# The first layer's last five pairs of blocks of batches 1 to 7 in 128x128 products, behind K0 to K2

## The chip, the cores and the metric

The kernel runs on one core of one Trainium2 chip. What counts is the device time of one execution in microseconds, taken as the median of several runs. A core has TensorE (PE; its weight loads are shown apart as PEld), VectorE (DVE), ScalarE (ACT), GpSimd (POOL) and SyncE (SP, which here only issues DMAs). Each engine takes its own instructions in a fixed order, and they wait for each other by semaphores.

## The reference

Attention with normalised queries and keys, and behind it two layers of a perceptron with a tanh GELU between them:

```python
q_n, k_n = rmsnorm(q, g_q), rmsnorm(k, g_k)          # (8, 12, 448, 64)
scores = scale * (q_n @ k_n.transpose(0, 1, 3, 2))
attn = softmax(scores)                               # over the keys
x = (attn @ v).transpose(0, 2, 1, 3).reshape(3584, 768)
h = x @ w_in                                         # 768 -> 2048
g = gelu_tanh(h)
out = g @ w_out                                      # 2048 -> 768, float32
```

## The kernel before

The work goes batch by batch, eight of them with 448 rows each. Within batch b TensorE makes the scores of 12 heads, the sums of the exponentials and the products with v, which give `xT[b]`: six slices (c = 0 to 5) of 128 inputs by 448 rows. Then comes the **first layer** of that batch: 2,048 outputs in 16 blocks of 128, two to a pair, so eight pairs K0 to K7. A pair needs 2 x 6 products of 128x128 weights by 448 rows. Its sums lie in two PSUM banks, and a GELU on ScalarE (line 532) takes them to `g` when the pair is complete. The **second layer** (`mm2`, the tiles `om`, `o` and `mm` with `wout`) of the batch ahead is cut into parts A to D and runs between the attention's steps. Batch 0 has an order of its own (`FRONT`), in which the first layer runs through `mm1` (line 523) in 128x128 products. In batches 1 to 7 nearly everything of TensorE is in 64x64 products (line 447).

Those are made by `Couple`. The array is used as four quarters of 64 rows by 64 columns. Two of a pair's accumulations run at one time: with `turn` 0 the upper half of the rows adds to bank 0 and the lower half to bank 1, with `turn` 1 the other way round. So one step of a couple, for one slice c and one turn, is four 64x64 products (a "four"), and a pair is 6 slices x 2 turns = 12 fours. [...] So where a couple changes its turn, `go` puts an empty order (line 456, `turned.nop()`) on another engine's queue, in the first layer on ScalarE's: it waits for the couple's last product, and the couple's next product waits for it (`gate`):

```python
if turned is not None:
    self.gate = turned.nop()
    after_all(self.gate, self.last)
```

The order of a batch is written out in `STEPS`, one text for each of the batches 1 to 4; batches 5 and 7 use 3, batch 6 uses 4. What stands behind "|" is the stretch with the first layer. There `k2:1:3-4!` is pair 2, turn 1, slices 3 up to but not 4, with a change of turn behind it ("!"). `A` to `D` with a number are that many fours of the second layer, `S`, `R`, `x` and `X` belong to the sums and products of the heads 8 to 11, which give slices 4 and 5, and `h` with a letter calls work that is hung there: `hg` the load of the GELU table, `hs` squares on ScalarE, `h-` and `hx` work of POOL and VectorE. More work is hung on the end of single blocks (`after(f)`, f = 0 to 15): loads, squares and sums of the batch two ahead, transposes of the next one, in batch 1 (f = 7) two table loads and a logarithm.

A pair's banks are one of three places (tile `hh`), given in turn to scores, sums and pairs; the pairs named in the text's second word (K3 and K7 in batch 1, K4 in 2, K3 in 3, K2 in 4) use the two single banks `o` and `mm` in their stead.

Of the kernel before, what the change touches and what calls it, by code (L numbers as in the profile page):

```python
# [16 lines left out]
def kernel(  # L17
# [596 lines left out]
    def m2_parts(b):  # L614
# [26 lines left out]
    homes = []  # L641

    STEPS = {
# [4 lines left out]
    }  # L648
    work = {}

# [6 lines left out]
    def run(b, text, m2, call, after):  # L657

        w = work.setdefault(b, dict(n=0, a=0, but=(), k={}))
        for token in text.split():  # L660
            kind, at = token[0], token[1:]
# [19 lines left out]
            elif kind in "Sx" and at[1] == "0":  # L681
# [6 lines left out]
                k = sums_couple(b, c, t, w["but"]) if kind == "S" else x_couple(b, c, t)  # L688
                w[token[:2]] = k, t, home
                k.go(0, range(4))  # L690
            elif kind == "x":
                w[token[:2]][0].go(0, range(4, NS))
            elif kind in "RX":
                j = "po".index(at[1])
                hp, of = 2 * int(at[0]) + j, ("S" if kind == "R" else "x") + at[0]
                _, t, home = w[of]
                oas[kind == "X"] = t[j]
                if kind == "X":
                    pair_x(b, hp)
                elif at.endswith("A"):  # L700
                    recips_by_logs(hp)
                else:
                    pair_recips(hp)
                w[of + "left"] = w.get(of + "left", 2) - 1
                if w[of + "left"] == 0 and home is not None:
                    leave(home)
            elif kind == "h":
                call(at, None)
            elif kind == "k":
                i, turn, at = token[1:].rstrip("!").split(":")  # L710
                i, turn = int(i), int(turn)
                lo, hi = (int(t) for t in at.split("-"))
                if i not in w["k"]:
                    w["k"][i] = mm1_couple(b, [2 * i, 2 * i + 1], f"K{i}" in w["but"])
                w["k"][i].go(turn, range(lo, hi), nc.scalar if token.endswith("!") else None)
                if w["k"][i].left == [0, 0]:
                    if f"K{i}" in w["but"]:
                        for k in range(2):
                            hs1[2 * i + k] = w["k"][i].tiles[k].rearrange("p (o s) -> p o s", o=1)
                            gelu(b, [2 * i + k])  # L720
                    else:
                        gelu(b, [2 * i, 2 * i + 1])
                    for f in (2 * i, 2 * i + 1):
                        after(f)
            else:
                raise ValueError(token)
# [230 lines left out]
    for b in range(B):  # L957
# [67 lines left out]
        def after(f):  # L1025
            for fn in m1.get(f, ()):
                fn()
# [53 lines left out]
```

## Time and profile before

| | |
|---|---|
| median of 3 runs | 402.72 us (401.46 to 403.55) |
| the profiled execution | 400.14 us |
| its span, first to last instruction | 398.1 us, mean granted clock 0.994 |
| first layer and what stands with it in the text, batch 1 | from about 80 to 100 us |
| the same in batch 3 | from about 171 to 192 us |
| the same in batch 7 | from about 353 to 374 us |

The page gives each engine's busy time, slices of the span, the chain of work that ended last, and groups of instructions by line and tile. The waits, the timeline and the windows are answers from the same trace. A row of the timeline joins instructions of one kind that follow each other: start, length of the whole row, engine, line, operation, tile and count, and in brackets the idle time ahead of it with what ended it. A TensorE product is shown with its whole passage through the array (0.35 us for 448 columns), so rows overlap; what sets the pace is the distance between starts.

### The profile page before, as it was taken

The page shows a single profiled execution, that of the slowest core. Times are in us where ns is not written, and L with a number is a line of the kernel's source. Part 1 is how long each engine was busy: PE and PEld are TensorE (multiplying, and loading weights), DVE is VectorE, ACT ScalarE, POOL GpSimd, SP SyncE. Part 2 cuts the span into 40 slices and gives each one's busy share as a digit, 9 for nine tenths or more (in the row PEclk, how much of TensorE's full clock was granted, in tenths as well). Part 3 has the DMA queues.
Part 4 walks back from the last instruction along what each step waited for, and adds up shares of the span by engine and source line. Part 5 has one row for each costly group of instructions (what it writes and reads, how often), then busy time and mean ns, then how long its engine had stood idle before and what let it go on. Part 6 is the DMA issues. An engine that isn't in the chain of part 4 may idle for free.

```text
span 398.1 us, 16991 instructions
## 1 busy us (share of the span) xinstructions
PE 388.9 (98%) x7572; PEld 285.5 (72%) x7572; DVE 243.7 (61%) x409; ACT 304.1 (76%) x409; POOL 137.8 (35%) x166
## 2 busy tenths in 40 slices
PE   7899999999999999999999999999999999999996
PEld 3444557878887678766788888776788889776664
DVE  5889829994897456864489635882399503690010
ACT  4897889968999779976997559985999258984400
POOL 5789002151321772155501646246420740000000
PEclk9899999999999999999999999999999999999999
DMA  8999999997947892939683398749743291210022
GB/s 181 227 237 204 205 204 213 242 252 133 166 105 151 204 192 33 216 84 214 85 160 104 91 215 104 162 130 200 105 66 90 76 122 28 68 56 3 2 81 79
DMA packets 75800, 54.63 MB, mean 137 GB/s; under 512 B 41680, under 2 KB 72272, under 8 KB 75728
## 3 DMA queue, kind: packets, MB, share of 16 engines
q1 hardware_dynamic: 59968, 41.69, 49.7%
q0 software_dynamic: 15440, 11.80, 20.3%
q8 instruction: 59, 0.97, 1.1%
q14 instruction: 13, 0.11, 0.1%
q10 hardware_dynamic: 320, 0.07, 0.1%
HBM read 45.61 MB, written 11.01 MB: 142 GB/s over the span
## 4 chain that ended last, share of the span: by engine, by line
PE 94%; ACT 2%; DMA 1%; SPq 1%; DVE 1%; issue 0%; ACTq 0%; DVEq 0%; POOLq 0%
PE hh L447 27%; PE om L447 17%; PE o L447 13%; PE mm L447 10%; PE sc L335 7%; PE o L552 5%; PE hh L523 4%; PE so L447 4%; ACT ex L326 1%; PE sc L351 1%; PE ox L386 1%; DMA rawk<-in_k_dram 1%; PE o L386 1%; PE h L523 1%; PE tp L266 1%; PE tp L259 1%
## 5 line engine op out<-in xcount | busy, mean ns | idle before, releaser
L326 ACT ACTIVATE ex<-sc,shift 128x896 bf16<-128x896 f32 x168 | 156.8, 1015 | 3.7 <-PE sc L351 2.1
L447 PE MATMUL hh<-xT,win 64*64 64x448 bf16 x2304 | 129.8, 349 | 0.7 <-issue 0.7
L447 PEld LDWEIGHTS <-g 64*64 64x64 bf16 x3072 | 108.4, 107 | 21.4 <-POOLq L456 1.2
L447 PEld LDWEIGHTS <-win 64*64 64x64 bf16 x2688 | 94.5, 106 | 33.7 <-ACTq L456 10.9
L447 PE MATMUL om<-wout,g 64*64 64x384 bf16 x1664 | 103.5, 322 | 0.0
L447 PE MATMUL mm<-wout,g 64*64 64x384 bf16 x704 | 86.0, 323 | 0.1
L447 PE MATMUL o<-wout,g 64*64 64x384 bf16 x704 | 85.2, 323 | 0.3 <-ACT g L532 0.3
L532 ACT ACTIVATE g<-hh 128x896 bf16<-128x896 f32 x55 | 49.7, 915 | 34.2 <-PE hh L447 31.7
L224 DVE TENSOR_REDUCE ss<-sq 128x14 f32<-128x896 f32 (+4 forms) x45 | 48.0, 1081 | 27.5 <-ACT sq L207 27.4
L362 DVE TENSOR_TENSOR es<-es,ex 128x896 bf16<-128x896 bf16 x92 | 57.0, 620 | 9.9 <-ACT ex L326 4.1
L335 PE MATMUL sc<-qT,kT 64*64 64x448 bf16 x600 | 57.0, 352 | 0.1
L920 POOL COPY mark<-es 1x1 bf16<-1x1 bf16 x27 | 8.9, 329 | 129.9 <-DVE es L362 109.4
L247 POOL TENSOR_TENSOR nrmq<-rawq,rinv 112x512 bf16<-112x512 f32 x35 | 36.4, 1054 | 30.7 <-DMA qT<-nrmq 23.7
L247 POOL TENSOR_TENSOR nrmk<-rawk,rinv 128x512 bf16<-128x512 f32 (+1 forms) x34 | 32.1, 959 | 2.3 <-ACT rinv L233 1.3
L362 DVE TENSOR_TENSOR es<-ex 128x896 bf16<-128x896 bf16 x21 | 12.9, 612 | 30.6 <-ACT ex L326 30.3
L447 PE MATMUL o<-xT,win 64*64 64x448 bf16 x192 | 31.5, 349 | 0.0
L447 PE MATMUL mm<-xT,win 64*64 64x448 bf16 x192 | 31.3, 349 | 0.0
L335 PEld LDWEIGHTS <-kT 64*64 64x64 bf16 x600 | 24.5, 106 | 8.3 <-issue 2.4
L300 DVE TENSOR_SCALAR kT<-kT,gcol 128x896 bf16<-128x896 bf16 x19 | 14.8, 777 | 23.7 <-DMA kT<-nrmk 23.7
L447 PEld LDWEIGHTS <-vt 64*64 64x64 bf16 x588 | 20.5, 107 | 6.2
L447 PE MATMUL o<-ex,vt 64*64 64x448 bf16 x182 | 20.8, 349 | 0.0
L447 PE MATMUL mm<-ex,vt 64*64 64x448 bf16 x182 | 20.5, 349 | 0.0
(112 smaller groups left out, 451.3 us busy)
## 6 DMA issues: line engine op xcount, KB each, us to landing
rawq<-in_q_dram SPq DMA_DIRECT2D x48, 224.0 KB, 5.2
rawk<-in_k_dram SPq DMA_DIRECT2D x42, 224.0 KB, 5.3
vt<-in_v_dram POOLq DMA_DIRECT2D x24, 168.0 KB, 4.3
win<-in_moe_w_in_dram POOLq DMA_DIRECT2D x4, 768.0 KB, 12.0
wout<-in_moe_w_out_dram POOLq DMA_DIRECT2D x4, 768.0 KB, 20.9
out_dram<-osb SPq DMA_DIRECT2D x7, 336.0 KB, 4.4
out_dram<-osb SPq DMA_DIRECT2D x8, 288.0 KB, 2.7
out_dram<-osb SPq DMA_DIRECT2D x8, 240.0 KB, 2.6
```

The costliest lines, as they stand in the source:

```text
L224: nc.vector.reduce_sum(stat(ssq[b % 3], b, c, n, j), view(n, sqs[n, b, c], j), axis=AX.X)
L247: eng.tensor_mul(dst.rearrange("p t a d -> p a t d"), view(n, raws[n, b, c], j), r.to_broadcast(list(r.shape) + [D]),)
L300: nc.vector.tensor_scalar(kT[:, c], kT[:, c], gcol[:, 0:1], None, op0=ALU.mult)
L326: latest[:] = [nc.scalar.activation(dst, sc[:, :, :S], AF.Exp, scale=scale, bias=shift)]
L335: nc.tensor.matmul(sc[own(j), a, :S], kT[own(a), c, t, own(j)], qT[b][own(a), 2 * c + j], start=True, stop=True,)
L362: nc.vector.tensor_add(es, exs[b, c, 0] if t == 1 else es, exs[b, c, t])
L386: nc.tensor.matmul(o[a * D:(a + 1) * D], w(a), e[:, a], start=(i == 0), stop=(i + 1 == len(steps)),)
L447: self.last = nc.tensor.matmul(self.outs[k][own(m)], w, e, start=not self.begun[k], stop=self.left[k] == 0,)
L523: nc.tensor.matmul(h[i * m:(i + 1) * m, j, :S], win[:, c // 2 + NCH * (c % 2), f * 128 + i * m:f * 128 + (i + 1) * m], xT[b][:, c], start= ...
L532: nc.scalar.activation(g[:, fs[0]:fs[0] + len(fs), (b % 2) * S:(b % 2 + 1) * S], hs1[fs[0]][:, :, :S], AF.Gelu_apprx_tanh)
L552: nc.tensor.matmul(o[j * m:(j + 1) * m, :HD], g[:, f, i * 128 + j * m:i * 128 + (j + 1) * m], wout[:, f, half * HD:(half + 1) * HD], start ...
L920: nc.gpsimd.tensor_copy(mark, x)
```

## The change

In the four texts the pieces of K3 to K7 are taken out, and the five words `k3 k4 k5 k6 k7` stand at the end. The pieces of K0 to K2 keep their order. `hs` and `hx` move by a few pieces in some batches. A word without ":" calls `mm1`: one pair after another, 12 products of 128x128 each, with the GELU and the hung work behind it. Nothing changes its turn there.

```diff
--- before.py
+++ after.py
@@ -641,10 +641,10 @@
     STEPS = {
...
-        2: '=oDDD,sDAP,oAAP,sAAA -K4 B4 ... k2:1:0-1! k3:1:3-4! k5:0:5-6 k2:0:0-1! k3:0:2-3 k5:0:4-5! k3:0:3-4 k2:1:2-3 k4:1:1-2! ...
+        2: '=oDDD,sDAP,oAAP,sAAA -K4 B4 ... k2:1:0-1! k2:0:0-1! k2:1:2-3 k3 k4 k5 k6 k7',
...
@@ -706,6 +706,12 @@
+            elif kind == "k" and ":" not in at:
+                i = int(at)
+                for fs in ([2 * i], [2 * i + 1]) if f"K{i}" in w["but"] else ([2 * i, 2 * i + 1],):
+                    mm1(b, fs)
+                for f in (2 * i, 2 * i + 1):
+                    after(f)
```

The end of the pieces of K0 to K2 in the new texts, from the piece on where something was taken out behind it:

```
1:        k0:0:4-5! k2:1:3-4 k0:1:2-3 k2:1:4-5 k0:1:5-6 hs k1:0:4-5 k2:1:5-6 k0:1:1-2 k0:1:0-1!
          k2:1:1-2 k0:0:5-6! k2:1:2-3 k2:1:0-1! hx k0:1:4-5 k1:0:2-3! k2:0:2-3 k1:1:4-6 k2:0:5-6
          k2:0:4-5 k3 k4 k5 k6 k7
2:        k0:0:5-6! k1:1:4-5! k0:1:4-5 k2:0:5-6! k0:1:5-6! k2:1:3-4 k1:0:5-6 k1:0:3-4 k2:1:1-2!
          k0:0:4-5 k1:0:1-2! k2:0:4-5 k1:1:1-2! k2:0:3-4! k1:0:4-5 k2:1:5-6 k2:1:4-5 k2:1:0-1!
          k2:0:0-1! k2:1:2-3 k3 k4 k5 k6 k7
3, 5, 7:  k1:0:4-5! k0:0:4-5! k2:0:0-1! k1:1:4-5! k2:1:0-1 hs k0:1:4-5 h- k2:1:2-4! k0:1:5-6
          k1:0:5-6! k2:0:4-5! k1:1:5-6 k2:1:4-5! k1:1:2-3 k1:1:1-2 k1:1:0-1 k2:0:3-4! k2:1:1-2
          k2:1:5-6 k3 k4 k5 k6 k7
4, 6:     k1:0:2-3! h- k1:1:4-5 k2:1:4-5 k1:1:2-3! k2:1:1-2 k0:0:5-6 k1:0:5-6! hx k2:1:3-4!
          k1:1:5-6 k2:0:2-3 k2:0:4-5 k2:0:3-4 k2:0:0-1 k3 k4 k5 k6 k7
```

In batch 3 before, the pieces from k2:1:2-4! on were: k2:1:2-4! k0:1:5-6 k1:0:5-6! k2:0:4-5! k3:1:1-2 k1:1:5-6 k2:1:4-5!. In batch 4 before: k0:0:5-6 k1:0:5-6! k3:1:0-1! k2:1:3-4! k1:1:5-6.

How TensorE's order changes at a change of turn: batch 2, from the end of k2:1:0-1! to the start of k2:0:0-1!. In the names, hh_3075 is K2's tile before, hh_3185 K3's and hh_3242 K5's; xT and win are the inputs and the weights of the first layer. Before:

```order
L447 MATMUL hh_3075<-xT_2574,win_127 64x448
L447 LDWEIGHTS win_127
L447 MATMUL hh_3185<-xT_2574,win_127 64x448
...
L447 LDWEIGHTS win_127
L447 MATMUL hh_3242<-xT_2574,win_127 64x448 [waits Activation_49]
...
L447 LDWEIGHTS win_127 [waits Activation_sequencer_49]
L447 MATMUL hh_3075<-xT_2574,win_127 64x448
```

After, where hh_2881 is K2's tile:

```order
L447 MATMUL hh_2881<-xT_2380,win_127 64x448
L447 LDWEIGHTS win_127 [waits Activation_sequencer_49]
L447 MATMUL hh_2881<-xT_2380,win_127 64x448
L447 LDWEIGHTS win_127
L447 MATMUL hh_2881<-xT_2380,win_127 64x448
```

The row that waits for ScalarE's queue stood behind a four of K3 and a four of K5; now it stands next to the product that ScalarE's order waits for.

The end of K2 in the same batch on TensorE, where mm_3104 and o_3103 are K4's banks before and hh_3006 is K3's tile after. Before:

```order
L447 MATMUL hh_3075<-xT_2574,win_127 64x448
L447 LDWEIGHTS win_127
L447 MATMUL mm_3104<-xT_2574,win_127 64x448
L447 LDWEIGHTS win_127
L447 MATMUL mm_3104<-xT_2574,win_127 64x448
L447 LDWEIGHTS win_127
L447 MATMUL o_3103<-xT_2574,win_127 64x448
```

After:

```order
L447 MATMUL hh_2881<-xT_2380,win_127 64x448
L523 LDWEIGHTS win_127
L523 MATMUL hh_3006<-xT_2380,win_127 128x448 [waits Activation_49]
L523 LDWEIGHTS win_127
L523 MATMUL hh_3006<-xT_2380,win_127 128x448
L523 LDWEIGHTS win_127
L523 MATMUL hh_3006<-xT_2380,win_127 128x448
```

A four of K4 followed K2's last four; now the first whole product of K3 follows it. In all, TensorE's order has 15,146 rows before and 12,626 after; the activations and copies of ScalarE, and VectorE's instructions, are the same in kind and number but for the tiles of K3 and K7 in batch 1, K3 or K4 in the others, which `mm1` calls `h` instead of `o` and `mm`.

8 rows, old and new, of the table STEPS are left out of this document.

## The prediction

> **What bounds the kernel now.** I read part 1 and part 4 of the page first, then the windows of 10 us, then the list of waits, and last the timeline at single places.
>
> ```profile
> PE 388.9 (98%) x7572; PEld 285.5 (72%) x7572; DVE 243.7 (61%) x409; ACT 304.1 (76%) x409; POOL 137.8 (35%) x166
> PE 94%; ACT 2%; DMA 1%; SPq 1%; DVE 1%; issue 0%; ACTq 0%; DVEq 0%; POOLq 0%
> 140.00:150.00 10.00, 10.00 (x224) 7.49 (x219) 5.04 (x4) 7.74 (x12) 7.48 (x6) 1.00 1.09 197
> 230.00:240.00 10.00, 10.00 (x220) 8.38 (x215) 3.76 (x3) 6.58 (x11) 4.72 (x5) 1.00 1.16 198
> 360.00:370.00 10.00, 10.00 (x220) 6.68 (x216) 0.00 (x0) 4.30 (x6) 0.00 (x0) 1.00 0.01 2
> ```
>
> The columns of a window are its length, then the busy time of PE, PEld, DVE, ACT and POOL with their counts, the granted clock, the DMA share and GB/s. TensorE is 94% of the chain that ended last, and the three windows lie in the first layers of batches 2, 4 and 7: TensorE is busy without a gap there at full clock, while ScalarE has 2 to 6 us to spare in each. So a stretch of first layer takes what its products take, and nothing else can be made shorter there. A busy TensorE is not yet one at its peak; that is read from the rate:
>
> ```profile
> 49.23 2.27 PE hh L523 x12
> 51.50 2.28 PE h L523 x12
> 366.54 7.19 PE hh L447 x152
> ```
>
> These are rows of the chain of waits (start, length, what). The 64x64 products run in fours, one for each quarter of the array: 152 of them are 38 fours, and 7.19 / 38 = 0.189 us for a four. Batch 0's first layer already runs in 128x128 products: 2.27 / 12 = 0.189 us for one. Four quarters and one whole product do the same work, in the same time.
>
> **The part that is replaced.** A pair of blocks is 12 products of 128x128 or 48 of 64x64. Five pairs in each of seven batches are 35 pairs: 35 x 36 = 1,260 matmuls and 1,260 weight loads fewer, which are the 2,520 rows that leave TensorE's order. Array time: 35 x 12 x 0.189 us before, and the same after. I cost this at **0**. The weight loads must stay hidden for that:
>
> ```profile
> L523 PEld LDWEIGHTS <-win 128*128 128x128 bf16 x96 | 9.1, 98 | 8.9 <-issue 1.1
> L447 PEld LDWEIGHTS <-win 64*64 64x64 bf16 x2688 | 94.5, 106 | 33.7 <-ACTq L456 10.9
> ```
>
> A 128x128 load takes 98 ns, and 12 products of batch 0 still come every 0.189 us, so the load lies beside the product ahead of it. In the open it would cost 420 x 0.098 = 41 us; this is a rival below.
>
> The GELU of a pair lies beside the next pair:
>
> ```profile
> L532 ACT ACTIVATE g<-hh 128x896 bf16<-128x896 f32 x55 | 49.7, 915 | 34.2 <-PE hh L447 31.7
> ```
>
> It takes 0.92 us and a pair 2.27 us, so it ends well before its bank is wanted: with three places, K6 takes the one that K2 or K3 left. The late squares on ScalarE and the table loads of batch 1 fit into what is left (1.35 us a pair), since they are the same ones as before. The last GELU of a batch follows K7 now as before, so the next batch's exponentials begin as they did. No term here.
>
> **What is taken away from K0 to K2: their cover.** A couple of 64x64 products swaps its two banks at each "!". There the next product of that couple waits until ScalarE has seen the last one land. The pieces of K3 to K7 that stood between did not wait for anything; they kept TensorE at work. The list of waits shows how often a weight load waited for ScalarE's queue, and the timeline of batch 3 how long a release takes:
>
> ```profile
> PEld L447 <- ACTq L456: 11.4, 72, 0.2
> 178.81 0.94 PE L447 MATMUL hh<-xT,win 64*64 64x448 bf16 x16
> 178.86 1.03 ACT L207 ACTIVATE sq<-rawk 128x448 f32<-128x448 f32 x2
> 179.30 0.22 PEld L447 LDWEIGHTS <-win 64*64 64x64 bf16 x8 [0.16 <-ACTq L456]
> 179.67 0.11 PEld L447 LDWEIGHTS <-win 64*64 64x64 bf16 x4 [0.16 <-ACTq L456]
> ```
>
> The 16 products at 178.81 are four fours, at 178.81, 179.00, 179.19 and 179.38. By the table they are the last of k2:1:2-4!, then k0:1:5-6, k1:0:5-6! and k2:0:4-5!. The last is behind the gate of the first; its weights load at 179.30, so the release takes 179.30 - 178.81 = 0.49 us from the start of the four ahead of the gate. Two fours between give 3 x 0.189 = 0.57 us: covered, with 0.08 us to spare. The same once more: k1:0:5-6! at 179.19, released at 179.67. In batch 4 the release is 0.51 us:
>
> ```profile
> 226.81 0.79 PE L447 MATMUL hh<-xT,win 64*64 64x448 bf16 x12
> 227.51 0.98 PEld L447 LDWEIGHTS <-win 64*64 64x64 bf16 x24 [0.15 <-ACTq L456]
> ```
>
> (the second of three fours, at 227.00, is k1:0:5-6!; the load at 227.51 is that of k1:1:5-6). So with **one four** between, the next starts at 0.49 to 0.51 in place of 0.38 us: 0.11 to 0.13 us are lost. With **none** between, 0.49 to 0.51 in place of 0.19: 0.30 to 0.32 us. I take 0.13 and 0.32, the upper ones, since the array has to fill again after a stop.
>
> Going through the new table piece by piece, a stop also gives time to the gates that are open beside it. Batch 1: one four between before k0:1:2-3, k0:0:5-6! and k1:1:4-6, so three ones. Batch 2: ones before k0:1:4-5, k2:1:3-4, k1:1:1-2! and k1:0:4-5 (k2:1:5-6 is covered by the stop ahead of it); none before k2:0:0-1! and before k2:1:2-3. Batches 3, 5 and 7 (one table): ones before k2:1:0-1 and k1:1:5-6 (k2:1:4-5! is covered by that stop), none before k2:1:1-2. Batches 4 and 6: none before k1:1:4-5, a one before k1:1:5-6 (k2:0:2-3 is covered). That is 3 + 4 + 3x2 + 2x1 = 15 ones and 2 + 3 + 2 = 7 nones: 15 x 0.13 + 7 x 0.32 = **4.2 us**. Bounds: 15 x 0.11 + 7 x 0.30 = 3.8 us, and with a whole four lost each time 15 x 0.19 + 7 x 0.38 = 5.5 us. All gates of K0 to K2 whose pieces between are unchanged (the first ones, beside the second layer and the sums) cost nothing, as before. Behind a waiting load stand all of TensorE's later products, for its order is fixed; so a stop is lost whole, as TensorE has no slack in these stretches to give it back.
>
> **The seams.** After K2 the array goes from quarters to one piece, and after K7 back. Both steps are in the trace of before once:
>
> ```profile
> 53.42 0.35 PE L523 MATMUL h<-xT,win 128*128 128x448 bf16 x1
> 53.70 0.38 PE L335 MATMUL sc<-qT,kT 64*64 64x448 bf16 x4
> 373.36 0.37 PE L447 MATMUL hh<-xT,win 64*64 64x448 bf16 x4
> 373.66 0.34 PE L552 MATMUL o<-wout,g 128*128 128x384 bf16 x1
> ```
>
> From the start of the last whole product to the first four it is 53.70 - 53.42 = 0.28 us in place of 0.19: 0.09 lost. From the last four to the first whole product it is 0.30 in place of 0.19: 0.11 lost, and 0.01 more in rounding. 0.21 us for both; batches 1 to 6 have both, batch 7's one step only moves from 373.66 to the end of K2. 6 x 0.21 = **1.3 us**. If work on both sides hid half of it, 0.6; if both gaps were lost whole, 6 x 0.58 = 3.5 us. I take the rows' difference, since they are the same two steps.
>
> **What moves otherwise.** K0 to K2 end about 1 to 2 us earlier (11 fours of K3 and K4 leave the space before K2's end in batch 3: 11 x 0.189 = 2.1 us, less the stops), so that the loads, transposes and squares hung on them are issued earlier on SP, POOL and ScalarE; those hung on K4 to K6 as well, as the pairs now end one after another. Nothing that TensorE waits for gets later. ScalarE loses the releases of K3 to K7; they took no time of TensorE, as the windows above show. One stop of TensorE with no visible cause stays where it is, ahead of the changed rows of batch 1:
>
> ```profile
> 85.42 0.37 PE L447 MATMUL hh<-xT,win 64*64 64x448 bf16 x1 [0.65 <-issue]
> ```
>
> **Sum.** 0 + 4.2 + 1.3 = 5.5 us. The profiled execution took 400.1 us (398.1 from first to last instruction and 2.0 around it): 405.6 us. That execution was 0.6% below the median of the runs shown, 402.7 us; a median after the change is to be set against that one: **408.2 us**, 1.4% slower.
>
> **Rivals.**
> *The releases are quicker than I take them* (no change). With fewer orders on ScalarE, or since the gated load goes ahead into a free quarter, a single four covers a gate and a none costs about half. Then 7 x 0.15 + 1.3 = 2.4 us, and if the stop of 0.65 us went as well, because TensorE has a sixth fewer instructions to fetch, 1.7 us: 404.4 us. It decides if a release is below 0.38 us. Against it: both releases above are 0.49 to 0.51 us, most of it the last product's own 0.35 us, and neither waited for ScalarE's work. Faster by more than 0.5% would need 2 us, and there is no such stop of TensorE in the first layers to be won.
>
> *The releases are slower* (412 us). ScalarE takes its orders in sequence; with K0 to K2 closer together, a release may stand behind GELUs or squares. Where four squares of 0.52 us stand ahead (batches 3 to 5) and GELUs of 0.92 us in all batches, one blocked release for each batch would cost some 0.5 us more, 7 x 0.5 = 3.5 us: 411.7 us. For it: the order; against it: the two squares at 178.86 ran until 179.89, and the releases at 179.30 and 179.67 came in between.
>
> *The weight loads come into the open* (449 us). If a whole-array product's weights could only be loaded when the product ahead is done, 420 loads of 98 ns would be added: 41 us. The rows of batch 0 speak against it, 0.189 us for each of 12 with a load each; only banks and data differ here. [...]
>
> **How the numbers follow.** My forecast 0.77; slower releases 0.11; weight loads in the open 0.01; quicker releases 0.09; some gain that I don't see 0.02. About 0.5%, 2 us, is what a measurement of this kernel tells from no change. Slower 0.77 + 0.11 + 0.01 = 0.89, same 0.09, faster 0.02. The likeliest case's bounds are 3.8 + 0.6 = 4.4 and 5.5 + 3.5 = 9.0 us, which is 407.1 to 411.7; the runs shown lie within 1.3 us of their median, and part of the quick releases belongs in: 404.8 to 411.8 us.
>
> **What would show it.** In the profile after: K3 to K7 at line 523 as 12 products in 2.27 us without a break (else the weight loads). Waits of PEld for ScalarE's queue fewer than 72, and those of K2's last pieces with an idle TensorE of 0.1 or 0.3 us behind them, 22 in all (else the gates were wrong). A step of 0.30 us at K2's end and of 0.28 us behind K7. I am wrong if TensorE is as closely packed in K0 to K2 as before, or if it waits for banks among K3 to K7 or at a batch's first scores.

## The result and the profile after

The median after the change is 406.52 us (405.51 to 408.00, 4 runs) against 402.09 us (401.44 to 403.55, 4 runs) of the kernel before, a ratio of 1.0106 with a 95% interval from 1.0072 to 1.0141: 4.4 us slower, between 2.9 and 5.7. The profiled execution took 408.0 us, with a span of 406.0 us.

Parts 1 and 4 of the page of the changed kernel:

```profile
PE 395.2 (97%) x6312; PEld 245.8 (61%) x6312; DVE 245.4 (60%) x409; ACT 306.2 (75%) x409; POOL 137.7 (34%) x166
PE 90%; ACT 3%; POOL 2%; DMA 2%; issue 1%; DVE 1%; SPq 0%; ACTq 0%; POOLq 0%; DVEq 0%
```

TensorE is still what the kernel waits for most. Its share of the chain that ended last has gone from 94% to 90%, but that is not the length of its stops. Followed back from a stop, the chain goes by the work that released it: in batch 2 it leaves TensorE from 127.4 to 140.3 us, though TensorE was busy for 12.33 us of the 12.40 from 127.4 on. The stops have to be read one by one. TensorE's products run at the same pace. These rows are from the chain of waits in batch 3 (start, length, what), K3 with the step ahead of it, and then K4 to K7:

```profile
184.63 2.38 PE h L523 x12
187.01 9.08 PE hh L523 x48
```

9.08 / 48 = 0.189 us for a whole product, as for a four before. Their weight loads take 98 ns each, as in batch 0 before, and lie beside the products (from 184.3 to 195.8 us TensorE is busy for 11.50 us of 11.50, with 5.79 us of weight loads in the same time):

```profile
L523 PEld LDWEIGHTS <-win 128*128 128x128 bf16 x516 | 49.7, 98 | 48.4 <-issue 3.4
```

The stops stand where K0 to K2 lost their cover. In the list of waits, weight loads wait for ScalarE's queue 50 times instead of 72, but for up to 0.5 us instead of 0.2 (us in total, times, longest):

```profile
PEld L447 <- ACTq L456: 12.8, 50, 0.5
```

The weight loads at the end of K2 in batch 2, from the timeline of the changed kernel:

```profile
139.18 0.12 PEld L447 LDWEIGHTS <-win 64*64 64x64 bf16 x4
139.84 0.11 PEld L447 LDWEIGHTS <-win 64*64 64x64 bf16 x4 [0.55 <-ACTq L456]
140.34 0.11 PEld L447 LDWEIGHTS <-win 64*64 64x64 bf16 x4 [0.39 <-ACTq L456]
140.66 0.11 PEld L523 LDWEIGHTS <-win 128*128 128x128 bf16 x2 [0.20 <-issue]
```

In the starts of the products there are 22 stops of TensorE ahead of such a load, at the pieces that the prediction lists. The loads at 139.84 and 140.34 belong to k2:0:0-1! and k2:1:2-3, two fours with a change of turn ahead of each and nothing between. They start 0.50 us apart instead of 0.19: the release takes what it took before, and 0.31 us of it are bare.

The steps of the array, in batch 3:

```profile
184.06 0.57 PE L447 MATMUL hh<-xT,win 64*64 64x448 bf16 x8
184.57 0.36 PE L523 MATMUL h<-xT,win 128*128 128x448 bf16 x1
195.17 0.92 PE L523 MATMUL hh<-xT,win 128*128 128x448 bf16 x4
196.02 0.36 PE L447 MATMUL om<-wout,g 64*64 64x384 bf16 x4
```

Eight products from 184.06 are the last two fours of K2, and the first whole product of K3 comes 0.51 us behind the first of them; without a step it would be 2 x 0.19 = 0.38 us, so 0.13 us are lost: 0.10 at the step, and 0.03 between the two fours, right behind the stop ahead of 184.06. On the way back the last of four whole products starts at 195.17 + 3 x 0.189 = 195.74, and the next four 0.28 us later.

**Stretch by stretch.** A stretch is a batch's first layer with what stands in its text behind "|", from the start of its first product to the start of the first product behind it, in us, read from the starts of the products in each profiled execution:

```
kernel                          batch 1   2      3      4      5      6      7     2 to 7 against before
before                           20.10  20.70  20.35  21.83  20.35  21.83  20.47
after                            21.06  22.04  21.13  22.51  21.25  22.51  21.03   +4.94
whole, K0-K2 covered             20.52  21.05  20.58  22.09  20.57  22.09  20.48   +1.33
fours, K0-K2 open                20.80  21.84  20.92  22.30  20.92  22.31  21.02   +3.78
fours, K0-K2 covered             19.39  21.08  20.36  21.83  20.35  21.83  20.47   +0.39
whole, covered, two steps more   21.71  21.29  20.80  22.32  20.80  22.32  20.71   +2.71
fours, covered, 21 orders, none  25.36  21.93  21.29  22.80  21.30  22.80  21.40   +5.99
fours, covered, 21 orders, one   22.25  21.37  20.73  22.18  20.73  22.24  20.83   +2.55
whole, covered, K0 first         19.34  20.93  20.58  22.09  20.57  22.09  20.48   +1.21
```

Batch 1 stands apart, because it holds a stop of TensorE that changes from execution to execution (last section). From before to after the seven stretches grow by 5.9 us; 0.35 us of that is this stop, which went from 1.00 to 1.35 us from product to product, and 0.12 us lie in the first four of batch 5, whose products came in two pairs 0.15 us apart; from then on batch 5 keeps pace with batch 3. The attention between the stretches is the same (174.34 and 174.32 us). The span differs by 7.9 us, of which 1.5 us lie ahead of batch 1's first score and 0.5 us behind TensorE's last product, where nothing was changed. So the stretches carry the change, and the times of whole runs scatter by about 2 us around it.

### The profile page after: what moved, and what is told of

It is laid out like the page before. It is cut to its first block, busy times and chain, and to the rows that moved or that the text cites. A ratio compares the mean times of both kernels' runs of the same rounds, so it can differ in the third digit from the quotient of the medians.

```text
span 406.0 us, 14370 instructions
## 1 busy us (share of the span) xinstructions
PE 395.2 (97%) x6312; PEld 245.8 (61%) x6312; DVE 245.4 (60%) x409; ACT 306.2 (75%) x409; POOL 137.7 (34%) x166
## 4 chain that ended last, share of the span: by engine, by line
PE 90%; ACT 3%; POOL 2%; DMA 2%; issue 1%; DVE 1%; SPq 0%; ACTq 0%; POOLq 0%; DVEq 0%
PE hh L523 20%; PE om L447 16%; PE o L447 12%; PE hh L447 9%; PE mm L447 7%; PE sc L335 7%; PE o L552 4%; PE h L523 4%; PE so L447 4%; ACT ex L326 1%; PE o L386 1%; PE ox L386 1%; DMA rawq<-in_q_dram 1%; PE sc L351 1%; POOL nrmq L247 1%
## 5 line engine op out<-in xcount | busy, mean ns | idle before, releaser
L447 PEld LDWEIGHTS <-g 64*64 64x64 bf16 x3072 | 94.8, 107 | 37.1 <-issue 3.4
L447 PE MATMUL om<-wout,g 64*64 64x384 bf16 x1664 | 100.6, 323 | 0.0
L447 PE MATMUL mm<-wout,g 64*64 64x384 bf16 x704 | 84.8, 323 | 0.1
L523 PE MATMUL hh<-xT,win 128*128 128x448 bf16 x432 | 83.9, 353 | 0.0
L523 PEld LDWEIGHTS <-win 128*128 128x128 bf16 x516 | 49.7, 98 | 48.4 <-issue 3.4
L447 PE MATMUL hh<-xT,win 64*64 64x448 bf16 x912 | 55.3, 352 | 1.8 <-issue 1.0
L335 PE MATMUL sc<-qT,kT 64*64 64x448 bf16 x600 | 55.2, 352 | 0.4 <-ACT ex L326 0.3
L447 PEld LDWEIGHTS <-win 64*64 64x64 bf16 x1008 | 30.9, 106 | 22.4 <-ACTq L456 12.3
L300 DVE TENSOR_SCALAR kT<-kT,gcol 128x896 bf16<-128x896 bf16 x19 | 16.8, 887 | 23.6 <-DMA kT<-nrmk 23.6
L335 PEld LDWEIGHTS <-kT 64*64 64x64 bf16 x600 | 21.5, 106 | 9.5 <-issue 2.3
```

The source lines that it names most:

```text
L300: nc.vector.tensor_scalar(kT[:, c], kT[:, c], gcol[:, 0:1], None, op0=ALU.mult)
L335: nc.tensor.matmul(sc[own(j), a, :S], kT[own(a), c, t, own(j)], qT[b][own(a), 2 * c + j], start=True, stop=True,)
L447: self.last = nc.tensor.matmul(self.outs[k][own(m)], w, e, start=not self.begun[k], stop=self.left[k] == 0,)
L523: nc.tensor.matmul(h[i * m:(i + 1) * m, j, :S], win[:, c // 2 + NCH * (c % 2), f * 128 + i * m:f * 128 + (i + 1) * m], xT[b][:, c], start= ...
```

## The experiments

The first three and the changed kernel make a square: K3 to K7 in whole products or in fours, K0 to K2 with or without two fours at every change of turn. The fourth adds steps of the array. All four were timed beside the same 21 runs of the kernel before, median 401.58 us.

**Whole products, K0 to K2 covered.** The edit, for batch 3 (the other texts alike):

```diff
-k0:0:4-5! k2:0:0-1! k1:1:4-5! k2:1:0-1 hs k0:1:4-5 h- k2:1:2-4! k0:1:5-6 k1:0:5-6! k2:0:4-5! k1:1:5-6 k2:1:4-5! k1:1:2-3 k1:1:1-2 k1:1:0-1 k2:0:3-4! k2:1:1-2 k2:1:5-6 k3 k4 k5 k6 k7
+k0:0:4-5! k2:0:0-1 k2:0:3-5! hs k1:1:0-3 h- k0:1:4-6 k1:1:4-6! k2:1:0-3 k1:0:5-6 k2:1:3-6 k3 k4 k5 k6 k7
```

> K3 to K7 in whole products as in the changed kernel, but the pieces of K0 to K2 put in another order, in which at least two fours stand between each change of turn and the couple's next product. Theory (open changes of turn cost 4.2 us, steps between quarters and whole array 1.3 us): 1.3 us above the kernel before, and in the seven first-layer stretches of the trace some 0.2 us more each (none in batch 7), with no idle TensorE ahead of a product that waited for ScalarE's queue. Rival A (the whole products themselves cost the time, by weight loads or banks): 4 to 5 us above before, as the changed kernel. Rival B (taking the pairs one after another, behind K2, costs it, by GELUs and hung work): also 4 to 5 us.

Measured: 403.46 us, ratio 1.0051 (1.0019 to 1.0082), 1.9 us slower. In batches 3 to 6 the stretches are 0.22 to 0.26 us above before, in batch 7 0.01 us. The list of waits has 19 short ones left, and no product of K0 to K2 waits for ScalarE's queue with TensorE idle:

```profile
PEld L447 <- ACTq L456: 3.1, 19, 0.2
```

Both rivals fall: the whole products are all there, one pair after another, and cost no more than the two steps. Most of what the changed kernel lost came back by the new order of K0 to K2. That order also has fewer changes of turn in K0 to K2, 68 in the seven batches instead of 91, as some pieces are joined. Their number is not the cause: the kernel before has the 91 too, and it is no slower than the third kernel below, which has 68.

**Fours behind K2, K0 to K2 open.**

```diff
-... k2:0:3-4! k2:1:1-2 k2:1:5-6 k3 k4 k5 k6 k7
+... k2:0:3-4! k2:1:1-2 k2:1:5-6 k3:0:0-6! k4:0:0-6! k3:1:0-6 k5:0:0-6! k4:1:0-6 k6:0:0-6! k5:1:0-6 k7:0:0-6! k6:1:0-6 k7:1:0-6
```

> K0 to K2 in the changed kernel's order, but K3 to K7 behind them in fours of 64x64, two pairs at a time, so that each of their changes of turn has six fours of cover. Theory: 4.2 us above the kernel before, with the 22 idle stretches of 0.1 or 0.3 us at the same pieces as in the changed kernel, and no steps at the end of K2 and K7. Rival A: no more than 0.5 us above before. Rival B: 4 to 5 us.

Measured: 405.23 us, ratio 1.0101 (1.0067 to 1.0134), 3.7 us slower. The stops are at the same pieces, and the list of waits has the same row as that of the changed kernel (12.8, 50, 0.5). The last stop of batch 3, ahead of k2:1:1-2, in the timeline:

```profile
181.32 1.62 PE L447 MATMUL hh<-xT,win 64*64 64x448 bf16 x24
182.36 0.52 PEld L447 LDWEIGHTS <-win 64*64 64x64 bf16 x16 [0.55 <-ACTq L456]
```

Six fours without a stop would be 5 x 0.189 + 0.35 = 1.30 us long; they take 1.62, so 0.32 us are lost. The stretches grow by 1.14 us in batch 2, 0.57 in 3 and 5, 0.47 and 0.48 in 4 and 6, 0.55 in 7. Here there is not one whole product behind K2: the form of K3 to K7 isn't what costs this.

**Both undone.** The covered order and the fours behind it.

> Both undone, but the place kept: K0 to K2 in the order with two fours or more at every change of turn, K3 to K7 behind them in fours. Theory: as the kernel before, within 0.5 us in the sum of the seven stretches. Rival A: as before. Rival B: 4 to 5 us above before, since K3 to K7 still come one after another behind K2.

Measured: 401.49 us, ratio 1.0008 (0.9986 to 1.0031). Batches 3 to 7 are as before to 0.01 us; batch 2 is 0.38 us longer, which I had not expected (see the last experiment). Taking the pairs one after another costs nothing.

**Two steps more.**

```diff
-k3 k4 k5 k6 k7
+k3 k4:0:0-6! k5:0:0-6! k4:1:0-6 k5:1:0-6 k6 k7
```

> As the first of these, but K4 and K5 in fours between whole products of K3 and of K6, K7: the array is changed over twice more in each of seven batches. Theory: 7 x 0.21 = 1.5 us more than the first, so 2.8 us above the kernel before, 0.21 us more in each of the seven stretches. If the change-over is hidden when the products behind it are ready: as the first.

Measured: 405.48 us, ratio 1.0108 (1.0055 to 1.0160), 3.9 us above before. Against the first experiment the stretches of batches 2 to 7 grow by 0.22 to 0.23 us each. Batch 4 in the timeline:

```profile
233.64 0.73 PE L523 MATMUL hh<-xT,win 128*128 128x448 bf16 x3
234.30 4.73 PE L447 MATMUL hh<-xT,win 64*64 64x448 bf16 x96
238.97 0.36 PE L523 MATMUL hh<-xT,win 128*128 128x448 bf16 x1
```

Three whole products at 233.64, 233.83 and 234.02, the first four 0.28 us behind; 24 fours would take 4.54 us, and the next whole product comes 4.67 us after the first of them. Nothing in these stretches waits for anything else at that place. The time is 1 us more than expected; batch 1 has most of that. Its stretch is 1.19 us longer than in the first experiment: 0.23 us for the steps, 0.29 us for its other stop, and 0.59 us where a change of turn of K4 fell behind the table loads on ScalarE (next).

**Orders that change nothing.** The kernel with both undone, with 21 empty orders more; then the same with one four between:

```diff
-k3:0:0-6! ... k5:0:0-6! ... k7:0:0-6!
+k3:0:0-3! k3:0:3-6! ... k5:0:0-3! k5:0:3-6! ... k7:0:0-3! k7:0:3-6!
```

```diff
-k3:1:0-6 k5:0:0-6! k4:1:0-6 k6:0:0-6! k5:1:0-6 k7:0:0-6!
+k3:1:0-3! k5:0:0-1 k3:1:3-6 k5:0:1-6! k4:1:0-3! k6:0:0-1 k4:1:3-6 k6:0:1-6! k5:1:0-3! k7:0:0-1 k5:1:3-6 k7:0:1-6!
```

> The kernel with both undone (K0 to K2 covered, K3 to K7 in fours behind) with 21 empty orders more, three a batch: one in the middle of the first turn of K3, K5 and K7, where nothing changes its turn, and the same couple goes on at once, with no four between. Theory: each costs 0.30 to 0.32 us of idle TensorE, 0.9 to 1.0 us in each of the seven stretches, 6.5 us in all. Rival (the stops in the changed kernel come from the banks or halves that really change over, not from the order's way there and back): nothing, since no bank changes.

> The same kernel with 21 empty orders more, each with one four of another couple between it and the couple's next product. Theory: 0.11 to 0.13 us each, 0.33 to 0.40 us in each of the seven stretches, 2.3 to 2.8 us in all. In batch 1 more where the order stands behind the table loads on ScalarE: up to the 0.6 us that one change of turn lost there in the kernel with two more change-overs. Rival as before: nothing.

Measured: 410.96 us (2 runs), ratio 1.0204 (1.0117 to 1.0292), and 405.94 us (8 runs), ratio 1.0072 (1.0033 to 1.0111), both beside a median before of 402.98 us. Against the kernel with both undone, batches 2 to 7 grow by 0.85 to 0.97 us with none between and by 0.29 to 0.41 us with one: 0.28 to 0.32 and 0.10 to 0.14 us for an order. Single loads behind such an order, in batch 3 of the first and of the second kernel:

```profile
187.82 0.33 PEld L447 LDWEIGHTS <-win 64*64 64x64 bf16 x12 [0.54 <-ACTq L456]
189.50 0.33 PEld L447 LDWEIGHTS <-win 64*64 64x64 bf16 x12 [0.36 <-ACTq L456]
```

At these orders the couple keeps its banks and its halves, so the price is that of the order's way to ScalarE and back. Batch 1 is another matter: the first kernel took 8.0 us more than before where 6.5 was forecast, and the excess lies there. Its loads and ScalarE in the timeline of the first of the two:

```profile
95.02 1.28 ACT L990 ACT_TABLE_LOAD   x1
96.32 0.34 ACT L230 ACTIVATE lg<-ss,eps 128x60 f32<-128x60 f32 x1
96.69 0.25 ACT L233 ACTIVATE rinv<-lg 128x60 f32<-128x60 f32 x1
96.77 1.36 PEld L447 LDWEIGHTS <-win 64*64 64x64 bf16 x32 [2.65 <-ACTq L456]
```

The order of K5 stood behind the logarithm and the exponential in ScalarE's sequence. The second began behind the first (96.32 and 96.69), the first behind its table load (95.02 to 96.30), and the release came at 96.77, when both had begun: one order without cover lost some 2.4 us. In the kernel with one four between, it was 1.3 us in the same stretch, over the 0.6 us that I had put down.

**K0 first in batch 2.**

```diff
-k2:0:3-6 k2:0:0-1! k0:1:4-6! k1:0:3-6 k1:0:1-2! k2:1:0-2 k0:0:4-5 k2:1:2-3 k1:1:1-2 k2:1:3-6
+k2:0:3-5 k0:1:4-6! k2:0:5-6 k2:0:0-1! k0:0:4-5 k1:0:3-6 k1:0:1-2! k2:1:0-2 k2:1:2-3 k1:1:1-2 k2:1:3-6
```

> The covered order with whole products, with K0 of batch 2 completed nine fours earlier. In the first such kernel K3's first product of batch 2 came 0.14 us later than the step alone explains. Theory: K3 waited there for the place that K0's GELU had to leave; now the step is 0.28 us as in the other batches, and batch 2's stretch falls by 0.1 to 0.15 us; the time is 1.5 us above the kernel before. Rival (that 0.14 us is part of the step): batch 2 as it was.

The edit completes K0 six fours earlier, not nine: its GELU starts 1.13 us earlier in the stretch, 6 x 0.189. Measured: 403.09 us, ratio 1.0002 (0.9967 to 1.0037). Batch 2's stretch falls by 0.12 us to 20.93, 0.23 above before like the others, and K3's first product comes 0.28 us behind K2's last one, instead of 0.42. In the first experiment the GELU of K0 had kept the place:

```profile
138.53 0.92 ACT L532 ACTIVATE g<-hh 128x896 bf16<-128x896 f32 x1 [1.63 <-PE hh L447]
```

It ended at 139.45, and K3's first product started at 139.50. The covered fours had the same order of K0 in batch 2: there K0's GELU ended at 137.87, K3's first product started at 137.92, and this stop of 0.27 us is most of their 0.38. The whole time came out equal to the kernel before where 1.5 us more was expected; the upper end of its interval is just that, and its batch 1 had none of the stop of 1 us, so the stretches are the better measure here. No version in this study is faster than the kernel before.

## Why the prediction was right

*TensorE bounds the first layer and has no slack:* every stop that was added is found again in the length of its stretch (with fours behind the open order 3.78 us in batches 2 to 7, for 3.80 us of stops).

*0 for the products, loads and GELUs:* shown. 0.189 us for each, and whole products behind covered pairs cost only the steps. The weight loads did not come into the open: 48 products with a load of 98 ns each took 9.08 us.

*4.2 us for the open changes of turn:* shown. The fours behind the open order give 1.14, 0.57, 0.47, 0.57, 0.48 and 0.55 us in batches 2 to 7; the prediction's prices make 1.16, 0.58, 0.45, 0.58, 0.45 and 0.58, together 3.80 against 3.78 measured. Batch 1 grew by 0.70 us, 0.29 of it its other stop: 0.41 against 0.39. The single prices, 0.13 and 0.32, lie in the 0.10 to 0.14 and the 0.28 to 0.32 us of the empty orders. My reason for the upper prices, an array that has to fill again after a stop, was not shown; measured is that the two fours behind the stop at 184.06 stand 0.03 us further apart than others.

*1.3 us for the steps:* shown. Set against the fours behind the same open order, the changed kernel has 0.19 to 0.22 us more in batches 2, 3, 4 and 6, where 0.21 was forecast. Behind the covered order it is 0.22 to 0.26 us a batch. Batch 7 has none, as predicted.

*The whole:* 4.85 us forecast for batches 2 to 7 of the changed kernel, 4.94 measured, of which 0.12 us are batch 5's first four, which the prediction has no term for. The time came out 1.7 us below the 408.2 us forecast: the median before was 0.6 us lower in this comparison, and 4.4 us of difference was measured with an interval that reaches to 5.7, so that 5.5 lies inside. Whole runs are the weaker test here; the stretches carry the sum.

*Quicker releases:* did not happen. In batch 2 the four without cover began 0.50 us after the one ahead of it (139.84 and 140.34), where less than 0.38 was needed, and the stop in batch 1 did not go with the rows that left TensorE's order (1.00 us before, 1.35 after, from product to product). That a gated load goes ahead into a free quarter was a guess, which no run shows.

*Slower releases:* did not happen in the changed kernel, where squares and GELUs on ScalarE held up no release. But they are real: in batch 1 of the first kernel with empty orders a release came behind orders on ScalarE that waited themselves, and 2.4 us were lost. My reason against it, two squares that ran on while releases passed, does not reach this far: there each square had begun before the release behind it came, and in batch 1, too, the release came only when the two activations had begun. The changed kernel has no change of turn at all behind K2, so nothing of it could wait there.

## What to carry to other kernels

In an order written out by hand, pieces of independent work may be the cover of a round trip between two engines (here 0.49 to 0.51 us). Before taking them out, measure that round trip from the trace and count for each wait how much work is left between; the loss followed here to a tenth of a microsecond for each batch. A form that needs no round trip (here whole products) did not pay, because the pieces that stayed lost their cover; they have to be put in a new order with it.

## What was not expected

The stop without a visible cause in batch 1, ahead of the changed pieces, changes between executions of nearly the same program up to there: from product to product it took 1.00 us before and 1.35 after, 0.41 in the covered fours, up to 1.49 with the empty orders, and none in the last kernel. That one lost time earlier, in batch 1's attention, where ScalarE waited for a load of q and TensorE for an exponential:

```profile
76.94 0.63 ACT L207 ACTIVATE sq<-rawq 112x512 f32<-112x512 f32 x1 [2.06 <-DMA rawq<-in_q_dram]
78.52 0.38 PE L335 MATMUL sc<-qT,kT 64*64 64x448 bf16 x4 [2.35 <-ACT ex L326]
```

The trace gives a lead on what the stop at 85 us waits for. Part 3 of the page has a DMA queue of the kind "instruction", with these packets, MB and share of time before and after:

```profile
q8 instruction: 59, 0.97, 1.1%
q8 instruction: 49, 0.80, 0.8%
```

59 packets for 15,146 rows of TensorE's order and 49 for 12,626 are 257 and 258 rows a packet, so my estimate is that these are the loads of TensorE's own instructions. In all eight kernels with the stop it ends at the same product, 1.46 to 1.78 us after the seventh packet has landed (83.64 and 85.42 us before, 86.07 and 87.52 after, 84.62 and 86.11 in the covered fours). In the last kernel the packet landed at 87.02 and TensorE came to that product 1.79 us later, without a stop. That TensorE waits there for its instructions is an estimate from these times; no run moves these loads alone, so it is not shown.

With the long wait in batch 1 of the first kernel with empty orders the granted clock fell as well. Windows of that kernel (after the five engines: clock, DMA share, GB/s):

```profile
97.00:98.00 1.00, 1.00 (x28) 0.64 (x24) 1.00 (x2) 1.00 (x1) 0.00 (x0) 0.96 0.01 2
98.00:101.00 3.00, 3.00 (x40) 1.57 (x36) 3.00 (x7) 1.17 (x2) 0.00 (x0) 0.50 0.42 82
101.00:104.00 3.00, 2.88 (x60) 1.55 (x56) 3.00 (x4) 0.92 (x1) 1.95 (x2) 0.95 0.86 189
```

From 98 to 101 us TensorE had half its clock (0.50, after 0.96 in the microsecond ahead and before 0.95 in the three behind), beginning about 1 us after it had gone on at 96.77. In those 3 us stand 36 weight loads, in the 3 us behind them 56. The length of the stop does not decide this alone. TensorE itself was idle for 2.23 us there (0.77 us busy from 94 to 97; the 2.65 us are those of its weight loads), and for 2.35 us in the last kernel, where the clock stayed at 1.00 from 75 to 86 us. The other execution of the first kernel had a mean granted clock of 1.000, so the fall does not come each time. What brings it is not shown here.
